# The second token group's up-projection as seven half-size products, in a fused attention and squared-ReLU kernel

## Chip, cores and metric

The kernel runs on one core of one Trainium2 chip. The metric is the device time of one execution in microseconds (us). TensorE (PE in the profile) does the matrix products, PEld is its loading of stationary operands, DVE is VectorE, ACT is ScalarE, POOL is GpSimd, SP is SyncE. POOL, SP and ACT also issue transfers (DMA).

## The reference

Attention with a linear distance bias and a window of 128 positions, then two dense layers with a squared ReLU between them:

```python
B, H, S, D = 8, 8, 576, 64
scores = matmul(q, k.T) / sqrt(D)                     # per batch and head
rel = pos[:, None] - pos[None, :]
scores = where((rel >= 0) & (rel < 128), scores - slope[h] * abs(rel), -1e9)
attn = softmax(scores)
x = (attn @ v).transpose(0, 2, 1, 3).reshape(4608, 512)
h = x @ w_in                                          # 512 -> 2048
g = maximum(h, 0) ** 2
out = g @ w_out                                       # 2048 -> 512, float32
```

## The kernel before

The 4608 tokens are nine groups of 512. A group is four blocks of 128 rows; a block is one batch and 128 positions (the last 64 positions of two batches share one). Matrices are bf16, sums are fp32 in PSUM, which has eight banks of 128 x 512 that all of PE's results share.

**Attention** of a block `m` is a chain of steps. `lk`, `lq`, `lv` (or `lkq`) load k, q and v by POOL. `tp m.0`, `tp m.1` transpose k and q on PE and `ev` evacuates them (from block 8 on, the transfer `kqT` does it on SP). `s m.0`, `s m.1` are the scores on PE, `e m.0` to `e m.3` the exponentials on ACT, `m m.0`, `m m.1` the multiplication with the mask on DVE, `pv m.0`, `pv m.1` the product with v on PE, `r` and `n` the reciprocal and the normalization on DVE, `xp m` the transposition of the result on PE and `x m` its evacuation (from block 13 on a transfer on SP). `mask*`, `pm*`, `one*`, `ident`, `dist*`, `slope*` are constants, built early.

**The up-projection** has two forms. The plain one (function `unit`, steps `u g.r.e`) multiplies w_in with the tokens: group 0 in four rows of 128 tokens, group 1 in two rows of 256 tokens and eight steps of two 128-column pieces each. Every step is followed by a ReLU on ACT (`relu`), which empties the PSUM bank, and a square (`sq`) on DVE or ACT.

The other form (`up_product`, steps `f g.u.p`) computes a group's 2 x 2 block product with seven half-size products instead of eight (Strassen's scheme in Winograd's form), for each quarter `u` of the columns. Products 1, 6, 7 and 4 add up in one bank, 2 has its own, 5 and 3 share one. Between them, partial sums are copied to SBUF (`s1`, `s2`, `s5` by `snap`, line 430 for ACT and 428 for DVE) and added (`c11`, `c22`, `c12`, line 1137, with the ReLU in the same instruction); the fourth result takes a plain ReLU after product 4. The scheme needs four sums of weight quarters for each `u` (`us u.0` to `us u.3`, line 1062; `us u.2` overwrites a part of w_in and so waits for every plain step) and four differences of the inputs for each group (`ut g.0` to `ut g.3`, line 1085). Products 1 and 2 read only the group's first 256 tokens, the others all 512.

**The down-projection** of each group (`product`, steps `p g.p.z`, line 1271) uses the same scheme on sums of g (`S1` to `S4`, line 1417) and of w_out (`ws`, line 1229); `s1_g`, `c11_g` and so on combine, `st` stores.

**Order.** Nothing is scheduled at run time. `ORDER` is a text with one item for each step: name, engine (`a` ACT, `d` DVE, `g` POOL, `s` SP, none for PE) and the numbers of the buffers it takes, PSUM banks for PE steps. Each engine executes its items in this order, waiting where an input or a buffer isn't there yet. `G_UP` says how many groups are plain:

```python
def ups(g):
    if g >= G_UP:
        return [("up", g, u, p) for u in range(4) for p in (1, 2, 6, 5, 7, 3, 4)]
    ...
    return [("unit", g, r, e) for r, (_, _, steps) in enumerate(UNITS[g]) for e in range(len(steps))]
...
tops = [x for gg in range(G_UP) for x in g_up[gg]]     # up_weight_sums: what us u.2 waits for
```

Of the kernel before, what the change touches and what calls it, by code (L numbers as in the profile page):

```python
# [69 lines left out]
reluu0.0.0:a:0 u0.2.0::6 mask0.3:a mask1.2:a mask0.1:a mask1.6:a e3.1:a u0.1.0::3 u0.1.1::0 pv3.0::1 pv3.1::5  # L70
u0.2.1::4 u0.0.2::7 squ0.0.0:d one1.2:d reluu0.1.0:a:0 mask0.2:a reluu0.2.0:a:1 one1.8:d r3.0:d squ0.1.0:d one1.7:d
r3.1:d n3.0:d n3.1:d xp3.0::5 x3.0:d one1.5:d reluu0.2.1:a:0 one1.6:d squ0.2.1:d squ0.2.0:d reluu0.1.1:a:2 mask1.5:a
mask1.4:a mask0.7:a mask0.5:a mask1.3:a mask1.0:a reluu0.0.2:a:3 u0.1.2::0 tp4.0::5 tp4.1::7 ev4.1.0:d squ0.0.2:d
u0.2.2::4 ev4.0.0:a reluu0.0.1:a:1 s4.0::7,2 s4.1::5,1 reluu0.1.2:a:0 e4.0:a lk5:g reluu0.2.2:a:3 lk6:g lq5:g lv5:g
lq6:g w_in4:g tp5.0::0 u0.0.3::6 u0.3.0::4 tp5.1::7 squ0.0.1:d one1.1:d one1.0:d squ0.1.2:d ev5.0.0:d e4.1:a mask0.0:a
mask0.4:a mask0.6:a m4.0:d ev5.1.0:d squ0.1.1:d lk7:g lv4:g lv6:g lq7:g w_out3:g w_out0:g lv7:g w_out2:g w_out1:g
e4.3:a reluu0.3.0:a:0 e4.2:a reluu0.0.3:a:1 squ0.3.0:d u0.3.1::2 tp6.0::7 reluu0.3.1:a:0 ev6.0.0:d tp6.1::4 s5.0::5,1
ev6.1.0:d one1.4:d one1.3:d squ0.0.3:d s5.1::6,0 u0.3.2::7 e5.0:a s6.0::5,4 s6.1::2,3 e5.1:a e5.3:a e6.0:a e5.2:a
# [5 lines left out]
u1.0.6::4 u1.0.4::2 reluu1.0.4:a:2 squ1.0.4:a u1.0.1::6 reluu1.0.0:a:1 squ1.0.0:a xp6.0::2 pv7.1::0 r7.1:d pv7.0::5
r7.0:d n7.0:d n7.1:d u1.0.7::1 u1.0.5::7 lkq8:g lkq12:g kqT8:s kqT12:s lkq9:g kqT9:s lkq10:g xp7.0::0 x7.0:a u1.0.3::5
S2.0.0:d x6.0:d reluu1.0.7:a:1 squ1.0.7:d us1.0:d us1.1:d us3.1:d reluu1.0.1:a:2 u1.1.6::0 reluu1.0.6:a:0
reluu1.1.6:a:1 squ1.0.6:a squ1.0.1:d us2.1:d reluu1.0.2:a:3 reluu1.0.3:a:0 squ1.0.2:a u1.1.3::1 u1.1.1::4 u1.1.4::0
reluu1.1.4:a:2 pm1:d pm2:d ws0.0:d squ1.0.3:a u1.1.5::5 u1.1.2::0 squ1.1.6:a reluu1.1.2:a:1 squ1.1.2:d S1.0.1:d
reluu1.1.3:a:0 S2.0.1:d squ1.1.4:a u1.1.0::3 u1.1.7::0 reluu1.1.1:a:1 squ1.1.1:a pm0:a us3.3:d us1.3:d reluu1.1.5:a:1
reluu1.1.0:a:2 squ1.1.5:a reluu1.0.5:a:3 squ1.0.5:a p0.2.0::1 p0.2.1 p1.1.0::4 p0.1.0::6 p1.1.1 p0.1.1 us0.2:d ws1.0:d  # L90
ws0.1:d ws0.3:d S3.0.1:d p0.5.0::7 ws0.2:d us2.3:d us0.3:d ws1.1:d ws1.3:d us2.2:d S4.0.1:d S4.0.0:d p0.5.1 squ1.1.0:d
S1.1.0:d ws1.2:d s1_0:a:0 p0.6.0 p0.6.1 s1_1:a:1 squ1.1.3:a s5_0:a:2 reluu1.1.7:a:0 squ1.1.7:a c11_0:d S2.1.0:d
us3.2:d S1.1.1:d us1.2:d s8.1::0,3 s8.0::5,2 s2_0:a:3 e8.0:a e8.3:a e8.1:a e8.2:a p0.3.0 p0.3.1 s9.1::3,1 s9.0::2,5
p0.7.0 p0.7.1 e9.0:a e9.3:a e9.2:a e9.1:a lv8:g lv9:g lv10:g kqT10:s s10.0::1,2 s10.1::3,0 lkq13:g lkq15:g lkq14:g
lv12:g lkq16:g lv13:g lv14:g kqT13:s kqT15:s c12_0:d S2.1.1:d m8.1:d m8.0:d c22_0:d p1.2.0::5 p1.2.1 m9.1:d e10.0:a
e10.1:a e10.3:a e10.2:a c11_1:d S3.1.0:d m10.1:d m9.0:d s12.1::0,2 s12.0::1,7 p0.4.0 pv8.0::5 pv8.1::3 r8.0:d r8.1:d
n8.0:d m10.0:d n8.1:d e12.0:a e12.3:a e12.1:a e12.2:a kqT14:s kqT16:s p1.6.0 p0.4.1 s3_0:a:4 pv9.0::2 pv10::7,5 r9.0:d
m12.1:d n9.0:d pv9.1::0 r9.1:d n9.1:d r10.0:d m12.0:d n10.0:d p1.6.1 xp8.0::2 p1.5.0::6 pv12.1::0 pv12.0::3 xp9.0::7
s2_1:a:5 p1.5.1 x8.0:a x9.0:a S3.1.1:d r12.1:d r10.1:d r12.0:d n12.0:d n10.1:d n12.1:d S4.1.1:d S4.1.0:d s13.0::3,7
s13.1::2,1 xp10.0::5 xp12.0::0 p1.7.0 p1.7.1 e13.0:a e13.1:a s5_1:a:6 e13.3:a e13.2:a m13.0:d x12.0:d x10.0:d ut2.0:d  # L100
s15.0::0,1 s14.0::7,3 s14.1::2,5 e15.0:a e14.0:a e15.1:a e14.2:a e14.1:a e14.3:a p1.3.0 p1.3.1 m13.1:d ut2.1:d c22_1:d
f2.0.5::1 pv13.1::2 pv13.0::3 m15.0:d c12_1:d ut2.2:d r13.0:d r13.1:d m14.0:d n13.0:d m14.1:d n13.1:d lkq17:g lv15:g
lv16:g lkq18:g st0.7.2:s st0.7.3:s st0.3.1:s kqT17:s st1.7.3:s st1.7.2:s st0.3.0:s s15.1::5,6 s16.0::7,0 e16.0:a
# [10 lines left out]
sqf2.3.4:a st1.2.1:s st0.2.0:s st1.3.1:s st0.2.1:s st1.2.0:s st1.3.0:s kqT18:s x14:s x13:s x15:s x16:s kqT20:s kqT21:s
kqT22:s s18.0::1,2 s18.1::0,7 p2.2.0::3 p2.2.1 S1.2.1:d S2.2.1:d r17.0:d S4.2.1:d S3.2.1:d r17.1:d n17.0:d e18.0:a
e18.1:a s1_2:a:3 S3.2.0:d n17.1:d m18.0:d p2.5.0::2 p2.6.0 p2.5.1 p2.6.1 f3.0.1::5 f3.0.2::4 f3.1.1::1 s2_2:d:7
e18.2:a e18.3:a s1.3.0:a:5 ut3.0:d ut3.1:d m18.1:d ut3.2:d c11.3.0:d:0 ut3.3:d c11_2:d f3.0.5::7 f3.0.6 s2.3.0:a:1
s5.3.0:a:0 s1.3.1:a:5 p2.7.0 f3.1.5::0 f3.0.7 s5.3.1:a:6 c22.3.0:d:3 f3.0.3 f3.1.6 s2.3.1:a:0 f3.1.3 s20.0::3,4
# [1362 lines left out]
```

## Time and profile before

| | |
|---|---|
| Time, median of 3 runs | 287.88 us (287.31 to 288.01) |
| The profiled execution, its own time | 288.0 us |
| Its span | 285.9 us, 8500 instructions |
| PE busy | 277.0 us (97%) |
| DVE busy | 247.1 us (86%) |
| ACT busy | 207.5 us (73%) |
| POOL busy | 106.3 us (37%) |
| DMA | 39.08 MB, mean 137 GB/s |

The span runs from the first to the last instruction; the rest of the time lies around it. The page gives the busy share of each engine, also in 40 equal slices of the span (one digit each, in tenths). Groups of instructions carry a count, the busy time of all, the mean duration of one in ns, and the idle time of the engine just ahead of them with what ended it. Consecutive instructions of an engine can overlap, so the distance between two starts is shorter than the duration.

### The profile page before, as it was taken

To read this page: it belongs to the slowest core of one execution; us is meant where nothing else is said; L and a number is where in the kernel's file an instruction comes from. 1 tells how busy PE (TensorE), PEld (TensorE's weight loads), DVE (VectorE), ACT (ScalarE), POOL (GpSimd) and SP (SyncE) were. 2 spreads that over 40 slices of the span, in tenths; PEclk is the share of its full clock that TensorE was granted. 3 is DMA by queue.
4 is the path that set the end of the run, shared out by engine and by line. 5 is a ranking of instruction groups with operands and counts; after the bars stand their busy time and mean duration, and the time that the engine had idled before them with its cause. 6 is when DMAs were issued, how large, how long until landed. Compare 5 with 4: busy or idle time off the path is not lost.

```text
span 285.9 us, 8500 instructions
## 1 busy us (share of the span) xinstructions
PE 277.0 (97%) x3403; PEld 240.0 (84%) x3404; DVE 247.1 (86%) x566; ACT 207.5 (73%) x408; POOL 106.3 (37%) x132
## 2 busy tenths in 40 slices
PE   6799999999999999999999999999999999999994
...
DVE  2555898799999999999999899998999979998752
ACT  4579978986588993879779958686898655657300
...
GB/s 126 161 197 167 183 201 165 171 172 148 206 145 250 131 172 129 149 207 130 203 135 150 139 174 164 170 164 157 148 93 39 40 73 3 0 111 39 53 79 127
DMA packets 169062, 39.08 MB, mean 137 GB/s; under 512 B 154560, under 2 KB 169024, under 8 KB 169024
## 3 DMA queue, kind: packets, MB, share of 16 engines
...
q1 hardware_dynamic: 53248, 20.00, 41.1%
q8 instruction: 26, 0.43, 0.7%
...
## 4 chain that ended last, share of the span: by engine, by line
PE 95%; ACT 2%; DVE 1%; issue 0%; POOL 0%; DVEq 0%; POOLq 0%
PE o L1271 38%; PE h L1116 30%; PE h L1021 9%; PE s L745 6%; PE pv L874 5%; PE wm L662 2%; PE xp L921 1%; PE tp L690 1%; ACT P L823 1%; ACT rt L988 1%; PE pv L856 1%; PE o L1373 0%; PE s L805 0%; ACT masks L475 0%; PE pv L851 0%; PE s L814 0%
## 5 line engine op out<-in xcount | busy, mean ns | idle before, releaser
L1271 PEld LDWEIGHTS <-g 128*128 128x128 bf16 x704 | 67.3, 98 | 9.0
L777 ACT ACTIVATE P<-s 128x512 bf16<-128x512 f32 x120 | 64.7, 613 | 5.7 <-PE s L745 3.3
L430 ACT ACTIVATE f<-h 128x512 f32<-128x512 f32 x74 | 42.5, 601 | 25.8 <-PE h L1116 25.5
L1137 DVE CUSTOM_DVE_ANT_0 rt<-h,f 128x512 bf16<-128x512 f32 x84 | 56.4, 684 | 4.9 <-ACT f L430 1.7
L980 ACT ACTIVATE g<-rt 128x512 bf16<-128x512 bf16 x79 | 48.4, 634 | 6.4 <-DVE rt L1137 5.9
L1271 PE MATMUL o<-w_out_sb,g 128*128 128x256 bf16 x432 | 52.3, 273 | 0.0
L1116 PE MATMUL h<-xT,w_in_sb 128*128 128x256 bf16 x336 | 46.9, 273 | 0.0
L1116 PEld LDWEIGHTS <-w_in_sb 128*128 128x128 bf16 x448 | 42.2, 98 | 5.6
L616 POOL DMA_DIRECT2D kq<-in_k_dram x24 | 21.5, 895 | 57.7 <-DMA kqT<-kq 54.7
L988 ACT ACTIVATE rt<-h 128x512 bf16<-128x512 f32 (+1 forms) x61 | 35.2, 599 | 8.6 <-PE h L1116 3.9
L1271 PE MATMUL o<-wsum,sums 128*128 128x256 bf16 x288 | 35.5, 273 | 0.0
L1116 PEld LDWEIGHTS <-us 128*128 128x128 bf16 x336 | 31.9, 98 | 4.3 <-DVE ut L1085 0.2
L1271 PE MATMUL o<-wsum,g 128*128 128x256 bf16 x272 | 34.5, 273 | 0.0
L772 DVE TENSOR_TENSOR P<-P,masks 128x1024 bf16<-128x1024 bf16 x48 | 32.2, 680 | 1.3 <-ACT masks L475 0.8
L1116 PE MATMUL h<-ut,us 128*128 128x256 bf16 x224 | 31.1, 273 | 0.0
L1021 PE MATMUL h<-xT,w_in_sb 128*128 128x128 bf16 (+1 forms) x384 | 30.8, 237 | 0.1
L982 DVE TENSOR_TENSOR g<-rt 128x512 bf16<-128x512 bf16 (+1 forms) x66 | 26.1, 413 | 4.7 <-ACT rt L988 4.4
L1271 PEld LDWEIGHTS <-sums 128*128 128x128 bf16 x288 | 27.5, 98 | 3.1
L901 DVE TENSOR_TENSOR x<-pv,rec 128x256 bf16<-128x256 f32 x72 | 28.7, 417 | 0.7
L1021 PEld LDWEIGHTS <-w_in_sb 128*128 128x128 bf16 x384 | 27.0, 98 | 2.3 <-issue 0.2
L621 POOL DMA_DIRECT2D vt<-in_v_dram x28 | 25.0, 908 | 7.8 <-PE pv L856 5.3
L430 ACT ACTIVATE f<-o 128x512 f32<-128x512 f32 x29 | 17.3, 599 | 11.0 <-PE o L1271 10.0
...
## 6 DMA issues: line engine op xcount, KB each, us to landing
...
w_out_sb<-in_moe_w_out_dram POOLq DMA_DIRECT2D x4, 512.0 KB, 11.6
w_in_sb<-in_moe_w_in_dram POOLq DMA_DIRECT2D x3, 512.0 KB, 8.6
...
```

The lines of the kernel that those rows point to most:

```text
L430: nc.scalar.activation(o, i, AF.Copy)
L621: nc.gpsimd.dma_start(tile_of(s_v[m])[0:n, :, 0:D], source(v, m))
L772: nc.vector.tensor_tensor(flat(Pt[sP.idx], w), flat(Pt[sP.idx], w), flat(mk, w), op=ALU.mult)
L777: nc.scalar.activation(flat(Pt[sP.idx], slice(2 * i, 2 * i + 2)), sS[i].tile.rearrange("p (j t) -> p j t", j=2)[:, :, lo:hi], AF.Exp, bias ...
L901: nc.vector.tensor_tensor(o, heads(sv)[0:n, :, 0:D], sr.tile[0:n, :].unsqueeze(2).to_broadcast([n, 4, D]), op=ALU.mult)
L980: nc.scalar.activation(o, i, AF.Square, bias=0.0, scale=1.0)
L982: nc.vector.tensor_tensor(o, i, i, op=ALU.mult)
L988: nc.scalar.activation(rts[srt.idx][:, 0:n], slot.tile[:, 0:n], AF.Relu, bias=0.0, scale=1.0)
L1021: nc.tensor.matmul(slot.tile[:, f * w:(f + 1) * w], w_in_sb[:, cc, fc * 128:(fc + 1) * 128], xT[:, cc, lo % (XR * 128):lo % (XR * 128) + w ...
L1116: nc.tensor.matmul(slot.tile[:, j * 256:j * 256 + 256], a, b_, start=fresh and j == 0 and c == 0, stop=c == 1, skip_group_check=True)
L1137: nc.vector._custom_dve(TENSOR_ADD_SAT, out=rts[srt.idx], in0=slot.tile, in1=other(), s0=FMAX, s1=0.0)
L1271: nc.tensor.matmul(slot.tile[:, z * 256:z * 256 + 256], stationary(c), moving(c), start=fresh and z == 0 and c == 0, stop=c == F - 1, skip ...
```

## The change

`G_UP` goes from 2 to 1: group 1's sixteen plain steps `u1.*` with their ReLUs and squares are replaced by the 28 products `f1.u.p` with their copies, sums, squares and the four input differences `ut1.*`; the weight sums `us` are needed before group 1's products, not before group 2's, and `us u.2` waits for group 0's plain steps only. The order is the same for the first 110 items and another one from there to the end, with other engines for some evacuations and squares and other banks.

```diff
-G_UP = 2
+G_UP = 1
...
 reluu0.0.0:a:0 u0.2.0::6 mask0.3:a mask1.2:a mask0.1:a mask1.6:a e3.1:a u0.1.0::3 u0.1.1::0 pv3.0::1
-pv3.1::5 u0.2.1::4 u0.0.2::7 squ0.0.0:d one1.2:d reluu0.1.0:a:0 mask0.2:a reluu0.2.0:a:1 one1.8:d r3.0:d squ0.1.0:d
-one1.7:d r3.1:d n3.0:d n3.1:d xp3.0::5 x3.0:d one1.5:d reluu0.2.1:a:0 one1.6:d squ0.2.1:d squ0.2.0:d reluu0.1.1:a:2
-mask1.5:a mask1.4:a mask0.7:a mask0.5:a mask1.3:a mask1.0:a reluu0.0.2:a:3 u0.1.2::0 tp4.0::5 tp4.1::7 ev4.1.0:d
-squ0.0.2:d u0.2.2::4 ev4.0.0:a reluu0.0.1:a:1 s4.0::7,2 s4.1::5,1 reluu0.1.2:a:0 e4.0:a lk5:g reluu0.2.2:a:3 lk6:g
-lq5:g lv5:g lq6:g w_in4:g tp5.0::0 u0.0.3::6 u0.3.0::4 tp5.1::7
...
-x5.0:d squ0.2.3:d pv6.1::0 r6.0:d squ0.3.2:d squ0.3.3:d S1.0.0:d s7.0::7,4 reluu0.1.3:a:1 r6.1:d e7.0:a e7.1:a m7.0:d
-us0.0:d s7.1::2,5 e7.3:a e7.2:a n6.0:d m7.1:d us3.0:d n6.1:d squ0.1.3:d us0.1:d S3.0.0:d us2.0:d u1.0.2::3 u1.0.0::7
...
+mask0.2:a reluu0.0.1:a:1 u0.2.1::2 pv3.1::5 lk5:g lq5:g one1.6:d mask0.4:a reluu0.1.0:a:2 squ0.1.0:d mask1.3:a
+mask0.5:a mask0.0:a u0.0.2::3 one1.1:d squ0.0.1:d one1.4:d one1.8:d one1.5:d mask1.4:a reluu0.2.0:a:3 mask1.5:a
+squ0.0.0:d r3.0:d r3.1:d n3.0:d n3.1:d reluu0.1.1:a:0 mask1.0:a reluu0.2.1:a:1 reluu0.0.2:a:2 mask0.6:a xp3.0::5
+u0.0.3::2 tp4.0::3 tp4.1::0 u0.1.2::1 w_in4:g lk6:g lk7:g lq6:g lv4:g lv5:g lv6:g lq7:g lv7:g ev4.0.0:a squ0.1.1:d
+squ0.2.0:d one1.2:d squ0.0.2:d squ0.2.1:d one1.3:d ev4.1.0:d x3.0:d s4.0::0,3 s4.1::5,6 tp5.0::4 ev5.0.0:d tp5.1::7
+reluu0.0.3:a:1 mask0.7:a reluu0.1.2:a:2 ev5.1.0:d squ0.0.3:d squ0.1.2:d e4.0:a e4.3:a e4.1:a m4.0:d u0.2.2::1 e4.2:a
+m4.1:d us0.0:d us1.0:d s5.0::6,7 s5.1::4,0 e5.0:a reluu0.2.2:a:2 e5.3:a e5.1:a u0.3.0::3 u0.3.2::6 reluu0.3.2:a:1
+e5.2:a reluu0.3.0:a:3 us3.0:d us2.0:d one1.0:d m5.0:d us1.1:d one1.7:d m5.1:d squ0.2.2:d us0.1:d u0.3.1::0 tp6.0::6
+tp7.0::7 tp6.1::1 u0.2.3::4 ev6.0.0:a ev6.1.0:a ev7.0.0:a reluu0.2.3:a:2 pv5.0::6 s6.0::1,3 pv5.1::5 tp7.1::7
+ev7.1.0:a e6.0:a e6.1:a pv4.1::4 pv4.0::2 r5.0:d us3.1:d n5.0:d r5.1:d squ0.3.0:d u0.0.4::6 r4.1:d n5.1:d r4.0:d
+n4.0:d squ0.3.2:d n4.1:d us2.1:d reluu0.0.4:a:3 m6.0:d S1.0.0:d squ0.0.4:d s7.0::1,5 s6.1::2,7 u0.1.3::3 s7.1::6,4
+e7.0:a e6.2:a e7.1:a m7.0:d e7.3:a e6.3:a m6.1:d xp4.0::1 pv6.0::2 u0.3.3::5 xp5.0::4 x4.0:a pv6.1::1 pv7.0::7 e7.2:a
+x5.0:a reluu0.1.3:a:3 reluu0.3.1:a:1 reluu0.3.3:a:0 w_out1:g w_out0:g lkq8:g lkq12:g w_out3:g w_out2:g kqT8:s kqT12:s
+lkq9:g lkq10:g lv8:g kqT9:s kqT10:s r6.0:d us0.2:d n6.0:d r6.1:d m7.1:d r7.0:d n6.1:d f1.1.2::4 f1.0.2::2 pv7.1::3
+n7.0:d r7.1:d squ0.3.3:d n7.1:d xp6.0::1 f1.1.1::0 f1.3.2::7 us1.2:d squ0.3.1:d x6.0:a s1.1.1:a:0 f1.3.1::3 xp7.0::1
+x7.0:a c11.1.1:d:0 f1.2.1::5 f1.0.1::6 f1.2.2::1 s1.1.2:a:0 s1.1.0:a:1 s1.1.3:a:2 us0.3:d ut1.0:d f1.0.5::4 ut1.1:d
+squ0.2.3:d f1.1.6 us2.2:d c11.1.0:d:2 ut1.2:d f1.0.6 sqc11.1.1:a s2.1.1:a:3 s2.1.0:a:1 s5.1.0:a:4 f1.3.6 f1.1.5::2
...
+f1.2.3 p0.1.0::2 f1.0.4 c22.1.2:d:2 S1.0.1:d S3.0.0:d reluf1.0.4:a:0 sqc22.1.2:a p0.1.1 sqf1.0.4:a c12.1.2:d:1
+c12.1.3:d:2 c22.1.3:d:0 S2.0.0:d f1.2.4 p0.5.0::6 p0.5.1 p1.1.0::7 s1_0:a:6 sqc12.1.2:a sqc22.1.3:a reluf1.2.4:a:1
...
```

More of the change, by code (lines that the diff above doesn't have):

```diff
@@ L69 @@
 n2.1:d u0.0.1::2 r1.0:d r1.1:d n1.0:d n1.1:d xp2.0::6 s3 u0.0.0::0 xp1.0::3 dist0:d x2.0:a e3.0:a x1.0:a mask1.7:a
[L70 to L78, printed above, removed]
@@ L84 @@
[L84 to L93, printed above, removed]
@@ L94 @@
[L94 to L103, printed above, removed]
@@ L114 @@
[L114 to L118, printed above, removed]
@@ L169 @@
-e37.2:a p5.3.0 p5.3.1 pv35.1::7 f6.3.1::4 f6.3.2::2 c22_5:d c12_5:d r35.1:d n35.1:d f6.2.1::3 s38.1::7,5 s38.0::0,1
-m37.0:d s1.6.3:a:2 e38.0:a e38.1:a e38.3:a c11.6.3:d:0 sqc11.6.3:d m37.1:d m38.0:d s1.6.2:d:2 p5.4.0 f6.3.6 f6.2.2::0
-f6.3.5::1 pv37.0::5 pv37.1::2 c11.6.2:d:0 s2.6.3:a:3 f6.3.7 r37.1:d f6.2.6 p5.4.1 f6.2.5::0 e38.2:a s5.6.3:a:1
-c22.6.3:d:2 m38.1:d r37.0:d n37.0:d n37.1:d s2.6.2:a:2 sqc11.6.2:a f6.2.7 f6.3.3 st4.4.3:s x31:s x32:s st5.2.1:s
-st5.2.0:s st4.3.0:s x33:s st4.3.1:s st4.4.2:s x34:s s5.6.2:a:1 c22.6.2:d:0 f6.2.3 sqc22.6.3:a sqf6.0.4:a c12.6.2:d:2
@@ L199 @@
-st8.4.1:s st8.4.0:s st8.3.0:a c21.1.128_8:d st8.4.1b:a
+reluu0.0.0:a:0 u0.2.0::6 mask0.3:a mask1.2:a mask0.1:a mask1.6:a e3.1:a u0.1.0::3 u0.1.1::0 pv3.0::1 mask0.2:a
+reluu0.0.1:a:1 u0.2.1::2 pv3.1::5 lk5:g lq5:g one1.6:d mask0.4:a reluu0.1.0:a:2 squ0.1.0:d mask1.3:a mask0.5:a
+mask0.0:a u0.0.2::3 one1.1:d squ0.0.1:d one1.4:d one1.8:d one1.5:d mask1.4:a reluu0.2.0:a:3 mask1.5:a squ0.0.0:d
+r3.0:d r3.1:d n3.0:d n3.1:d reluu0.1.1:a:0 mask1.0:a reluu0.2.1:a:1 reluu0.0.2:a:2 mask0.6:a xp3.0::5 u0.0.3::2
@@ new lines @@
+tp4.0::3 tp4.1::0 u0.1.2::1 w_in4:g lk6:g lk7:g lq6:g lv4:g lv5:g lv6:g lq7:g lv7:g ev4.0.0:a squ0.1.1:d squ0.2.0:d
+one1.2:d squ0.0.2:d squ0.2.1:d one1.3:d ev4.1.0:d x3.0:d s4.0::0,3 s4.1::5,6 tp5.0::4 ev5.0.0:d tp5.1::7
+reluu0.0.3:a:1 mask0.7:a reluu0.1.2:a:2 ev5.1.0:d squ0.0.3:d squ0.1.2:d e4.0:a e4.3:a e4.1:a m4.0:d u0.2.2::1 e4.2:a
+m4.1:d us0.0:d us1.0:d s5.0::6,7 s5.1::4,0 e5.0:a reluu0.2.2:a:2 e5.3:a e5.1:a u0.3.0::3 u0.3.2::6 reluu0.3.2:a:1
+e5.2:a reluu0.3.0:a:3 us3.0:d us2.0:d one1.0:d m5.0:d us1.1:d one1.7:d m5.1:d squ0.2.2:d us0.1:d u0.3.1::0 tp6.0::6
@@ new lines @@
+pm2:d r8.1:d r8.0:d m10.0:d S2.1.1:d s3_0:a:2 e12.0:a e12.3:a e12.2:a e12.1:a p1.5.0::2 pv9.1::0 p1.5.1 p1.6.0
+pv9.0::4 p1.6.1 s5_1:a:4 s2_1:a:3 m10.1:d S3.1.1:d m12.0:d r9.0:d n9.0:d r9.1:d n8.0:d n9.1:d pv12.0::1 pv10::4,3
+n8.1:d r12.0:d r10.0:d r10.1:d n10.0:d S4.1.1:d n10.1:d m12.1:d n12.0:d xp9.0::0 p1.7.0 kqT14:s x9.0:a s13.0::0,4
+s13.1::5,6 p1.7.1 e13.0:a e13.2:a e13.1:a pv12.1::0 xp10.0::3 xp8.0::5 x10.0:a e13.3:a x8.0:a r12.1:d n12.1:d m13.0:d
+p1.3.0 xp12.0::3 pv13.0::0 s15.0::6,4 s14.0::5,1 e14.0:a e15.0:a e14.1:a e15.1:a c22_1:d x12.0:d r13.0:d ut2.0:d
@@ new lines @@
+s5.2.3:a:7 f2.2.3 s17.1::0,3 f2.3.7 kqT18:s st0.3.1:s st1.7.3:s st0.2.0:s st1.3.0:s x14:s st1.7.2:s st0.2.1:s
+st0.3.0:s kqT20:s x15:s kqT22:s x16:s kqT21:s sqc22.2.2:d c22.2.3:d:2 sqc22.2.1:a c12.2.2:d:1 f2.3.3 p2.1.0::2
+c12.2.3:d:0 sqc12.2.2:d e17.3:a reluf2.2.4:a:3 sqf2.2.4:d e17.2:a sqc22.2.3:a f2.3.4 reluf2.3.4:a:2 sqf2.3.4:a p2.1.1
+pv17.0::4 sqc12.2.3:a s18.1::1,5 s18.0::0,6 e18.0:a e18.2:a s1_2:a:5 e18.1:a p2.2.0::3 p2.2.1 S1.2.0:d S2.2.0:d
+S1.2.1:d r17.0:d S2.2.1:d n17.0:d c11_2:d m17.1:d S3.2.1:d S3.2.0:d p2.5.0::1 p2.6.0 f3.0.1::3 s1.3.0:a:0 e18.3:a
```

191 lines of the change are left out of this document (103 added, 88 removed).

## The prediction

> **What bounds the kernel now.** I read the page first, then the stretches of time, the chain that ended last, the groups by shape and the timeline of the first 65 us.
>
> ```profile
> span 285.9 us, 8500 instructions
> PE 277.0 (97%) x3403; PEld 240.0 (84%) x3404; DVE 247.1 (86%) x566; ACT 207.5 (73%) x408; POOL 106.3 (37%) x132
> PE   6799999999999999999999999999999999999994
> DVE  2555898799999999999999899998999979998752
> ACT  4579978986588993879779958686898655657300
> ```
>
> The profiled execution took 288.0 us, 2.1 us of it outside the span; the median of the three runs is 287.88. TensorE is full from the fifth slice to the end, and VectorE nearly so from the ninth (56 us). Before that ACT has the fuller slices, the fifth and the sixth.
>
> ```profile
> 20.30:38.70 18.40, 17.95 (x358) 16.88 (x356) 13.97 (x48) 17.46 (x43) 12.51 (x15) 1.00 1.87 179
> 38.70:53.70 15.00, 15.00 (x153) 13.44 (x153) 11.90 (x31) 12.09 (x25) 7.61 (x10) 1.00 1.87 174
> 53.70:281.80 228.10, 228.10 (x2713) 199.21 (x2711) 212.64 (x454) 166.22 (x315) 68.48 (x82) 1.00 1.21 129
> 60.00:80.00 20.00, 20.00 (x302) 17.06 (x301) 19.71 (x45) 14.68 (x29) 14.13 (x19) 1.00 1.98 169
> ```
>
> The columns are length, then busy time of PE, PEld, DVE, ACT and POOL. The first stretch begins where the new order begins, the second holds the plain up-projection of group 1, the third starts with the first down product. From 53.7 on PE has no idle time at all. So whatever PE work goes is gained in full, and whatever PE waits is lost in full; nothing later makes it good. In the first stretch ACT is busy 95% and DVE 76%: what PE can meet there is ACT.
>
> ```profile
> 20.60 0.91 PE h L1021 x16
> 21.53 1.08 ACT rt L988 x2
> 22.61 1.18 ACT masks L475 x6
> 23.80 0.50 ACT rt L988
> 24.33 0.38 PE tp L690 x4
> ...
> 28.28 0.22 PE tp L690 x4
> 28.50 0.89 PE h L1021 x16
> ...
> 31.54 0.55 PE s L745 x16
> ...
> 33.98 0.97 PE pv L874 x32
> ...
> 38.67 4.47 PE h L1021 x40
> ...
> 53.77 8.73 PE o L1271 x80
> ```
>
> The chain leaves PE only once behind 20 us for longer: from 21.5 to 24.3 it runs over relus and six masks on ACT, because a transpose takes the PSUM bank that a relu behind those masks frees. From 38.67 (u1.0.2) it is PE alone. Eighty 256-column matmuls in 8.73 us make 109.1 ns each.
>
> **The change, part by part.**
>
> ```profile
> L1021 PE MATMUL h<-xT,w_in_sb 128*128 128x256 bf16 x128 | 14.6, 273 | 0.0
> L1137 DVE CUSTOM_DVE_ANT_0 rt<-h,f 128x512 bf16<-128x512 f32 x84 | 56.4, 684 | 4.9 <-ACT f L430 1.7 <-PE h L1116 1.1 <-ACT g L980 0.9
> L430 ACT ACTIVATE f<-h 128x512 f32<-128x512 f32 x74 | 42.5, 601 | 25.8 <-PE h L1116 25.5
> L988 ACT ACTIVATE rt<-h 128x512 bf16<-128x512 f32 x59 | 34.6, 607 | 8.6 <-PE h L1116 3.9 <-PE h L1021 2.0 <-DVE rt L1137 1.5
> L988 ACT ACTIVATE rt<-h 128x256 bf16<-128x256 f32 x2 | 0.8, 386 | 0.0
> ```
>
> *1. PE work.* Group 1's 128 plain matmuls go; 4 quarters of 7 products of 4 matmuls, 112, come, of the same shape. 16 x 109.1 ns = **1.75 us less**, all of it on the path.
>
> *2. Work on the other engines.* Relus of group 1 fall from 16 to 4, and 12 copies of partial sums into f (L430, 601 ns against 607) come: ACT is even. DVE gets 12 sums (L1137) and 4 input differences (ut). What an instruction costs in a row of its kind is the distance between starts:
>
> ```profile
> 19.94 0.60 ACT L988 ACTIVATE rt<-h 128x512 bf16<-128x512 f32 x1
> 20.19 0.41 PE L874 MATMUL pv<-vf,P 128*128 128x65 bf16 x8
> 44.24 0.76 DVE L901 TENSOR_TENSOR x<-pv,rec 128x256 bf16<-128x256 f32 x2
> 46.36 2.06 ACT L988 ACTIVATE rt<-h 128x512 bf16<-128x512 f32 x4
> 89.51 1.28 DVE L1137 CUSTOM_DVE_ANT_0 rt<-h,f 128x512 bf16<-128x512 f32 x2
> 97.73 0.75 DVE L982 TENSOR_TENSOR g<-rt 128x512 bf16<-128x512 bf16 x2
> ```
>
> ACT 512 wide: (2.06 - 0.61)/3 = 0.48 us. A mask: 1.18/6 = 0.20, from the chain above. DVE sum: 1.28 - 0.68 = 0.60; DVE 512 in bf16, and the norm: 0.75 - 0.42 = 0.33. So 12 x 0.60 + 4 x 0.33 = 8.5 us more on DVE, less five squares and a few evacuations that the new order gives to ACT (about 4 us). DVE's 86% rises by about 1.5 points. It must bear this, and the 16 weight sums (us) brought forward, between 30 and 60 us, where the second row of the stretches shows it 3.1 us idle.
>
> *3. The new order up to the first of group 1.* The shared 110 steps end with ACT free at 19.94 (row above) and PE at the second half of the pv row, 20.35. From there I walk the two lists. PE's next is u0.2.1 in bank 2, then pv3.1, u0.0.2, xp3, and **u0.0.3, again in bank 2**, which the relu of u0.2.1 has to free. PE's own work up to there is 0.12 + 2 x 0.89 + 0.22 = 2.1 us: it arrives at 22.5. ACT has ahead of that relu eight masks (1.6), three relus (1.44) and a half-wide one (estimate 0.27, from 386 against 607 ns): it starts at 23.25, lasts 0.61, and PE goes on at 23.95. **A wait of 1.45 us**; before, PE's idle time in the whole first stretch, this jam included, is 18.40 - 17.95 = 0.45 us.
>
> Queued behind u0.0.3 are tp4.0 and tp4.1, so ACT itself runs dry: free at 24.4, its next step evacuates tp4.0, which ends at 23.95 + 0.89 + 0.38 = 25.2. ACT restarts at 25.35. From there to x5.0, which evacuates the last input that products 1 and 2 read and frees the bank of f1.1.2, ACT's list holds 5 evacuations, 7 relus, 16 exponentials, x4.0 and a mask: 29 x 0.48 + 0.2 = 14.1 us, until 39.45; two short waits that the walk meets (0.15 for the relu of u0.3.2, 0.40 for the evacuation of tp7.1); x5.0 itself 0.60 and the way to PE 0.1. **f1.1.2 starts at 40.7.** In the old order x5 is DVE's, and u1.0.2 starts at 38.67 with the same PE steps behind it but for one half of values (8 matmuls, 0.24).
>
> *4. From there to the down products.* Before the first down product both orders put the same PE steps, but for 16 units of 8 matmuls (13.97 us) against 25 of the 28 products of 4 (10.91). From f1.1.2 on the new list has 11.6 us until then; ut1.0 waits for x7.0, and that for pv7.1, n7.1 and xp7.0, for which I add 0.3. First down product at 52.6, and the three products left over (1.31) make it the equal of 53.9. Before: 53.77. **So waits of some 1.9 us more eat the 1.75: +0.2.**
>
> *5. Switches to score matmuls.*
>
> ```profile
> 61.25 1.25 PE L1271 MATMUL o<-wsum,sums 128*128 128x256 bf16 x10
> 62.43 0.23 PE L745 MATMUL s<-kqT,kqT 64*128 64x128 bf16 x2
> ...
> 62.84 0.22 PE L745 MATMUL s<-kqT 64*128 64x128 bf16 x2
> 62.99 1.92 PE L1271 MATMUL o<-w_out_sb,g 128*128 128x256 bf16 x16
> ```
>
> Ten matmuls from 61.25 end at 62.34, the scores start at 62.43; on the way back the last pair at 62.84 would let the next start at 62.90, and it starts at 62.99. About 0.09 each way, 0.18 a visit. The old list visits scores 32 times, the new one 33: +0.2. [...]
>
> *6. Transfers.* In POOL's queue w_in4 moves ahead of three loads (lk6, lv5, lq6), and lkq8 and lkq12 ahead of w_out3 and w_out2.
>
> ```profile
> 22.58 0.75 POOL L543 DMA_DIRECT2D w_in_sb<-in_moe_w_in_dram  x1 [1.40 <-DMA w_in_sb<-in_moe_w_in_dram]
> 47.38 1.34 SPq L676 DMA_TRANSPOSE kqT<-kq  x1
> ...
> w_in_sb<-in_moe_w_in_dram POOLq DMA_DIRECT2D x3, 512.0 KB, 8.6
> ```
>
> Now it lands about 22.58 + 8.6 = 31.2. In the new list us0.0 reads it from about 29.5 us. Three places sooner are at least 3 x 0.8 us (106.3 us of POOL for 132 instructions): it lands by 28.8, and the step costs nothing; were it late, m5.0 stands behind us0.0 on DVE and pv5.0 behind that, 1.7 us at the old landing. kqT8 waits for all weights; four issues later are 3.2 us, 50.6 instead of 47.4, and the scores that read it run at 62.4 (row above) or later: 0. The order behind p0 moves without changing work, and the tail (last product, three sums, stores) is the same list: 0, if PE waits there as little as now.
>
> **Sum:** 288.0 + 0.2 (waits 1.95, work -1.75) + 0.2 (the visit) = **288.4 us**; against the median of 287.88 that is half a microsecond more. About 0.3% (0.86 us) is what a measurement of this kernel tells from no change, so this is none.
>
> **Rivals.** *A, faster: the walk overstates ACT.* Had ACT no idle time, x5.0 would start at 19.94 + 34 x 0.48 + 0.27 + 10 x 0.20 = 38.5 and f1.1.2 at 39.2, 1.5 us sooner: **286.9**. For it: 17.46 of 18.40 us busy now. Against: tp4.0 really stands behind u0.0.3.
>
> *B, slower: DVE becomes the pacer between m6.1 and p0.3.0.* That stretch of DVE's list is 12 sums, 6 S, 4 ws and 2 masks (24 x 0.60), 8 us, 4 ut, 4 squares and 4 norms (20 x 0.33) and 4 reciprocals: 21.4 us. m6.1 can start when e6.3 ends, 39.4, so S4.0.1 is there at 60.9; PE wants it 9.2 us behind its first product, at 61.8. The margin is 0.9 us. At the idle share of 60 to 80 us (1.5%) 0.3 us goes and nothing happens. It decides from 4% on; at 10%, half of what 38.7 to 53.7 shows (21%), 2.4 us go: **289.9**, and at 21% it would be some 293.
>
> *C, slower: waits further back.* The order is new as far as the end, and nothing in this trace shows it; the old one has PE without idle time from 53.7. Two or three waits at the size of the old order's early idle time (0.45) give **289.5**.
>
> *D: the products are not cheaper,* because a half-size product came with more per matmul: **290.1**. Against: groups 2 to 8 run them at 109 ns.
>
> **How the numbers follow.** Forecast 0.52 (its own range 287.6 to 289.2: 0.4 us either way for each of the two walked waits), A 0.14, B 0.20, C 0.12, D 0.02. Faster by over 0.3% (under 287.0): most of A, 0.12. Slower by over 0.3% (over 288.7): B, D, most of C and a fifth of the forecast, 0.43. Within: 0.45. The range runs from A to just behind B, 286.7 to 290.3.
>
> **What would show it.** Right: 896 matmuls where the products are issued (784 now), none of 256 columns among the plain ones; a PE wait near 22.5 to 24 that ends on ACT rt; f1's first matmul near 40.7 and the first down product near 52.6; no idle PE later. Wrong: f1 before 39.5 (A); p0.5, p0.6 or p0.3 (PE o from sums or g) waiting for a DVE sum between 55 and 62 (B); PE waits behind 62 (C).

## The result, and the profile after

The changed kernel took 290.01 us in the median (288.27 to 292.91), the kernel before 287.95 beside it (287.22 to 289.62): a ratio of 1.0056 with a 95% interval of 1.0033 to 1.0079, 0.56% slower (the execution of 292.91 us counts as slow and is not in the ratio). The forecast of 288.4 was 1.6 us too low; the time lies in its range, near its upper end. Repeated later, the ratio was 1.0061 (1.0032 to 1.009). No run of the changed kernel was under 288.27, and they spread over 3 us and more.

The profiled execution took 289.69 us. Its page, with the slices of PE and of its granted clock:

```profile
span 287.9 us, 8490 instructions
PE 278.3 (97%) x3388; PEld 239.9 (83%) x3388; DVE 250.4 (87%) x570; ACT 213.4 (74%) x420; POOL 106.3 (37%) x132
PE   6898999999999999999999999999999999999994
PEclk9979999999999999999999999999999999999999
```

The third slice of the clock shows a 7 (a 9 before). The stretches of time around it; behind the length of the stretch stands PE's busy time, and the third number from the end is the granted clock:

```profile
12.00:13.00 1.00, 0.49 (x10) 0.30 (x8) 0.60 (x2) 1.00 (x3) 1.00 (x2) 1.00 1.58 168
13.00:14.00 1.00, 0.53 (x12) 0.40 (x12) 0.62 (x4) 0.61 (x2) 1.00 (x3) 1.00 1.44 190
14.00:15.00 1.00, 0.52 (x10) 0.33 (x7) 0.81 (x3) 0.87 (x2) 1.00 (x3) 1.00 1.42 198
15.00:16.00 1.00, 1.00 (x17) 1.00 (x17) 0.51 (x3) 0.30 (x2) 1.00 (x2) 0.50 1.28 206
16.00:17.00 1.00, 1.00 (x8) 0.45 (x6) 1.00 (x6) 0.00 (x0) 1.00 (x2) 0.50 1.24 207
17.00:18.00 1.00, 1.00 (x12) 0.98 (x10) 0.97 (x5) 0.00 (x0) 0.49 (x1) 0.50 1.74 177
18.00:19.00 1.00, 1.00 (x18) 0.72 (x16) 0.04 (x1) 0.71 (x2) 0.00 (x0) 0.80 1.76 203
```

From 15.0 to about 18.4 us the clock was 0.50 (the mean of 0.80 in the last row makes 0.4 us at 0.50). That lies in the first 110 steps, which both kernels share: u0.1.1, one of the last of them on PE, ended at 22.12 us instead of 20.35 (an expectation below has 20.38 for it). So this profile is 1.8 us late before anything that the change touched begins. Behind that point, three rows of PE's timeline:

```profile
24.84 0.40 PE L924 MATMUL xp<-ident,x 128*128 128x128 bf16 x4 [0.42 <-DVE x L904]
25.68 1.05 PE L1024 MATMUL h<-xT,w_in_sb 128*128 128x128 bf16 x16 [0.45 <-ACT rt L991]
...
281.88 1.93 PE L1376 MATMUL o<-wsum,g 128*128 128x256 bf16 x24
```

The up-products in the groups by shape:

```profile
L1119 PE MATMUL h<-xT,w_in_sb 128*128 128x256 bf16 x384 | 53.4, 273 | 0.1
L1119 PE MATMUL h<-ut,us 128*128 128x256 bf16 x256 | 34.4, 273 | 0.0
L1119 PE MATMUL h<-xT,us 128*128 128x256 bf16 x128 | 19.2, 273 | 0.0
L1119 PE MATMUL h<-ut,w_in_sb 128*128 128x256 bf16 x128 | 18.7, 273 | 0.0
```

384 + 256 + 128 + 128 are the 896 product matmuls. The wait at u0.0.3 (25.68) is there, ended by the ReLU on ACT. The changed kernel's second profile (290.21 us) has no clock dip and is the one to read. From its PE timeline:

```profile
23.39 0.83 PE L1024 MATMUL h<-xT,w_in_sb 128*128 128x128 bf16 x12 [0.45 <-ACT rt L991]
...
34.23 0.40 PE L693 MATMUL tp<-ident,kq 128*128 128x128 bf16 x4 [0.59 <-DMA kq<-in_q_dram]
...
40.70 1.03 PE L1119 MATMUL h<-xT,w_in_sb 128*128 128x256 bf16 x8
...
112.70 1.48 PE L1119 MATMUL h<-ut,us 128*128 128x256 bf16 x12 [2.08 <-DVE ut L1088]
...
282.42 1.93 PE L1376 MATMUL o<-wsum,g 128*128 128x256 bf16 x24
```

From the chain of work that ended last in it:

```profile
26.03 8.16 DMA kq<-in_q_dram
34.23 0.40 PE tp L693 x4
...
35.16 1.08 ACT P L780 x2
36.24 0.49 ACT rt L991
36.73 2.45 ACT P L780 x5
39.18 0.49 ACT xT L433
39.67 0.49 ACT P L780
40.16 0.50 ACT xT L433
...
106.50 0.26 DVE x L904
106.76 5.34 DMA xT<-x
...
112.22 0.44 DVE ut L1088
...
112.70 2.83 PE h L1119 x24
```

And from SP's timeline, the issues of x15, kqT22 and x16:

```profile
100.46 2.49 SPq L911 DMA_TRANSPOSE xT<-x  x1
103.12 3.54 SPq L679 DMA_TRANSPOSE kqT<-kq  x1
106.76 1.22 SPq L911 DMA_TRANSPOSE xT<-x  x1
```

Two waits here were not in the prediction. tp7.1 waits 0.59 us for the load lq7, which lands at 34.19, and the chain from there runs over ACT to f1.1.2 at 40.70, the last 5.5 us of it on ACT without a break. The load alone is not the difference: in the kernel before lq7 landed no sooner (34.58), PE did not wait for it, and group 1 started 4.0 us behind it, here 6.5. And far behind, f3.0.5 waits 2.08 us: its input difference ut3.0 needs the transposed x of block 16. The last row of SP is that transfer, x16. Its input was ready at 100.2 (n16.1's end), but SP had kqT20, x15 and kqT22 ahead of it and issued it at 106.76; it landed at 112.10. In the old list x13 to x16 stand ahead of kqT20, n16.1 ends at 95.55, x16 is issued at 97.5 and lands at 103.35, some 7 us before ut3.0 starts at 110.55. So two things came together: x16's input is ready 4.6 us later (100.2 against 95.55), and its issue comes another 6.6 us behind that. (The DVE x ahead of it in the chain is n17.0, which ends at 106.89, behind that issue, and is not its input.)

The names of the lower rows belong to the experiments below. With these two points each profiled execution can be split at the first matmul of group 1 (u1.0.2 or f1.1.2) and at the end of the last product, in us. Column 3 counts from the end of u0.1.1, column 4 from group 1's first matmul; column 5 is the wait at f3.0.5 within column 4:

| kernel | end of u0.1.1 | to group 1 | to the end of PE | wait f3.0.5 | its time |
|---|---|---|---|---|---|
| before | 20.35 | 18.26 | 243.20 | 0 | 288.0 |
| changed, first profile | 22.12 | 20.19 | 241.50 | 0 | 289.69 |
| changed, second profile | 19.83 | 20.87 | 243.64 | 2.08 | 290.21 |
| masks later | 20.22 | 20.93 | 243.21 | 1.65 | 290.24 |
| x15, x16 ahead | 19.74 | 21.30 | 241.50 | 0 | 288.43 |
| x15, x16, lq7 ahead | 20.43 | 19.63 | 241.49 | 0 | 287.31 |
| before, with dummies | 20.01 | 18.26 | 243.20 | 0 | 287.31 |
| changed, with dummies | 20.59 | 20.38 | 241.48 | 0 | 288.33 |

The stretch behind group 1's start, without that wait, is 241.5 to 241.6 us in every kernel with the new order and 243.2 with the old one. The gain is there each time, 1.6 to 1.7 us. It goes again in three places: a start of group 1 that is 1.9 to 3.0 us later behind u0.1.1 (1.4 with lq7 ahead), a wait of about 2 us for x16 in some executions, and the clock, which hits both kernels (3.4 us at 0.50 in the first profile of the changed one, and in one of the kernel before with x16 moved).

### The profile page after: what moved, and what is told of

It is laid out like the page before. It is cut to its first block, busy times and chain, and to the rows that moved or that the text cites. A ratio compares the mean times of both kernels' runs of the same rounds, so it can differ in the third digit from the quotient of the medians.

```text
span 287.9 us, 8490 instructions
## 1 busy us (share of the span) xinstructions
PE 278.3 (97%) x3388; PEld 239.9 (83%) x3388; DVE 250.4 (87%) x570; ACT 213.4 (74%) x420; POOL 106.3 (37%) x132
## 4 chain that ended last, share of the span: by engine, by line
PE 92%; ACT 5%; DVE 1%; issue 1%; POOL 0%; DVEq 0%; POOLq 0%; ACTq 0%
PE o L1274 38%; PE h L1119 35%; PE s L748 6%; PE pv L877 4%; PE h L1024 3%; PE wm L665 2%; ACT P L780 1%; PE tp L693 1%; ACT masks L478 1%; PE xp L924 1%; ACT P L826 1%; ACT rt L991 1%; PE s L808 1%; ACT xT L433 1%; PE pv L859 1%
## 5 line engine op out<-in xcount | busy, mean ns | idle before, releaser
L1140 DVE CUSTOM_DVE_ANT_0 rt<-h,f 128x512 bf16<-128x512 f32 x96 | 64.0, 684 | 4.8 <-PE h L1119 2.9
L433 ACT ACTIVATE f<-h 128x512 f32<-128x512 f32 x87 | 50.1, 604 | 18.1 <-PE h L1119 14.4
L983 ACT ACTIVATE g<-rt 128x512 bf16<-128x512 bf16 x84 | 51.8, 634 | 6.6 <-DVE rt L1140 6.1
L1119 PE MATMUL h<-xT,w_in_sb 128*128 128x256 bf16 x384 | 53.4, 273 | 0.1
L1119 PEld LDWEIGHTS <-w_in_sb 128*128 128x128 bf16 x512 | 47.7, 98 | 6.6 <-DVE x L904 0.5
L1119 PEld LDWEIGHTS <-us 128*128 128x128 bf16 x384 | 36.9, 98 | 4.7 <-DVE ut L1088 0.2
L1119 PE MATMUL h<-ut,us 128*128 128x256 bf16 x256 | 34.4, 273 | 0.0
L991 ACT ACTIVATE rt<-h 128x512 bf16<-128x512 f32 (+1 forms) x49 | 28.5, 601 | 5.8 <-DVE g L985 2.9
L877 PEld LDWEIGHTS <-P 128*128 128x128 bf16 x448 | 20.6, 99 | 3.2 <-ACT P L826 1.3
L619 POOL DMA_DIRECT2D kq<-in_q_dram x24 | 21.8, 910 | 1.6 <-DMA w_out_sb<-in_moe_w_out_dram 1.6
```

The source lines that it names most:

```text
L433: nc.scalar.activation(o, i, AF.Copy)
L619: nc.gpsimd.dma_start(view(kq[s_kq[m].idx], i), source(src, m, split))
L877: nc.tensor.matmul(sv.tile[0:n, hi * (D + 1):(hi + 1) * (D + 1)], prob, tile_of(s_v[mk])[:, h, 0:D + 1], start=mk == parts[0][1], stop=mk ...
L983: nc.scalar.activation(o, i, AF.Square, bias=0.0, scale=1.0)
L991: nc.scalar.activation(rts[srt.idx][:, 0:n], slot.tile[:, 0:n], AF.Relu, bias=0.0, scale=1.0)
L1119: nc.tensor.matmul(slot.tile[:, j * 256:j * 256 + 256], a, b_, start=fresh and j == 0 and c == 0, stop=c == 1, skip_group_check=True)
```

## The experiments

**The changed kernel once more**, unedited.

> The changed kernel once more, nothing edited. In its first profiled execution the common prefix (the first 110 steps, up to u0.1.1) ended 1.74 us later than in the one of before (22.12 against 20.38), behind a granted clock of 0.50 from 15.0 to 18.4 us, and from there to the last product both took nearly the same (261.69 against 261.42 us). Theory 'clock' (the extra is the dip in the prefix, which the change only meets more often): this profile's time is 288.3 to 288.6 us if no dip is in it and 289.5 to 290 if one is, and prefix end to last product is again 261.7, within 0.2. Theory 'waits' (the new order's own waits make it slower): no dip, and still 289.5 or more, with over 262.8 us behind the prefix.

Median 289.65 us (288.62 to 292.43), before 288.23 beside it. No dip, and still 290.21 us in the profile: "clock" alone fell, "waits" held, with 264.5 us from u0.1.1 to the end of the last full product, 2.1 of it at one place that neither theory had named.

**The masks later on ACT.** Two squares on DVE, squ0.0.0 and squ0.0.1, come sooner as well; the lines show ACT's and PE's items.

```diff
-... mask0.4:a reluu0.1.0:a:2 squ0.1.0:d mask1.3:a mask0.5:a mask0.0:a u0.0.2::3 ... mask1.4:a reluu0.2.0:a:3 mask1.5:a
-... reluu0.1.1:a:0 mask1.0:a reluu0.2.1:a:1 reluu0.0.2:a:2 mask0.6:a xp3.0::5 u0.0.3::2
+... reluu0.1.0:a:2 squ0.1.0:d u0.0.2::3 ... reluu0.2.0:a:3 mask0.4:a ... reluu0.1.1:a:0 reluu0.2.1:a:1 mask1.3:a
+reluu0.0.2:a:2 mask0.5:a mask0.0:a mask1.4:a mask1.5:a mask1.0:a mask0.6:a xp3.0::5 u0.0.3::2
```

> The changed kernel with six of the masks on ACT behind the ReLU that frees u0.0.3's bank (and the two squares that free its buffers ahead on DVE); the work is the same. My theory of the early jam: u0.0.3 waits 0.2 us instead of 1.2 to 1.45, tp4.0 ends 1.2 us sooner and ACT no longer runs dry ahead of it; f1.1.2 and the first down product come 0.9 to 1.2 us sooner, and the time falls by 0.9 to 1.2 us against the changed kernel, to about 287.4 in undisturbed executions. Rival (ACT's total work, not its order, sets f1.1.2): the wait goes, but f1.1.2 stays within 0.3 us of the changed kernel's place behind the prefix. Theory 'clock' expects the spread between runs to stay.

Median 290.28 us (288.58 to 292.51): no gain. PE's timeline has u0.0.3 without a wait:

```profile
22.77 0.89 PE L1025 MATMUL h<-xT,w_in_sb 128*128 128x128 bf16 x13
```

The chain that ended last:

```profile
26.10 8.54 DMA kq<-in_q_dram
...
41.16 1.03 PE h L1120 x8
```

u0.0.3 came 2.55 us behind u0.1.1 instead of 3.56, a whole microsecond sooner, and f1.1.2 20.93 behind it instead of 20.87. PE met lq7's landing (34.64) all the same and waited there 0.67 us, and f1.1.2 came 6.5 us behind that landing as before. My theory of the early jam fell as a cause of the time: the jam is real, but a load stands behind it.

**Dummy products in PE's idle stretches**, in the changed kernel and in the one before. The dummies write a bank that the step behind them overwrites.

```diff
+BUSY = {'tp1.0': 3, 'pv2.0': 6, 'pv0.0': 8, 'xp0.0': 7}
...
     def fill(task, slot):
-        for _ in range(int(task.gap * FILL / 56.0) if task.gap > 400.0 else 0):
+        for _ in range(BUSY.get(task.name, 0)):
             nc.tensor.matmul(slot.tile[:, 0:128], warm[:, 0:128], warm[:, 0:128], start=True, stop=True)
```

> The changed kernel with 24 dummy products of 128 columns in four idle stretches of PE between 9.9 and 14.5 us (3, 6, 8 and 7 of them, ahead of tp1.0, pv2.0, pv0.0 and xp0.0, written into banks that the step behind them overwrites), so that PE is not idle there. Theory 'clock': the granted clock stays at 1.00 up to 280 us in every execution, the spread of 3 us falls to under 1, and the median falls from 290.0 to 288.3 to 288.6. Theory 'waits': the median stays at 289.5 to 290.

> The kernel before with the same 24 dummy products. Theory 'clock': its few slow runs (289.2 to 289.6 of 11) go and the median stays at 287.7 to 288.0, so that the changed kernel with dummies is 0.3 to 0.7 us slower than this one, as predicted. Theory 'waits': no change here, and the difference to the changed kernel with dummies stays at 1.6 us or more.

Changed: 288.89 us (288.33 to 289.98). Before: 287.79 (287.31 to 288.69). In 70 runs of the kernel before that stood beside these and the next experiments, 17 had a mean clock of 0.994, and those took 289.27 to 291.35 us; with the dummies none of the 24 was under 0.997. So with dummies in PE's idle stretches between 10 and 15 us the dip was not seen, and it makes most of the slow tail of the kernel before, 17 of its 19 executions above 289.2 us; the changed one reached 290.87 us with a clock of 1.00. The difference between the two with dummies is 1.1 us, between what the two theories expected. Without the dip and without dummies it is larger: the changed kernel's 15 executions of both measurements with a mean clock of 0.996 or more have a median of 289.69 us, the 26 of the kernel before beside the repeat 287.85. So the clock is part of the spread and no cause of the difference. That the dummies took 0.76 us from the changed kernel (289.65 to 288.89) is not shown to be the clock: in its profile x16 lands at 107.84 and f3.0.5 has no wait.

**x15 and x16 ahead on SP.**

```diff
-st1.7.2:s st0.2.1:s st0.3.0:s kqT20:s x15:s kqT22:s x16:s kqT21:s
+st1.7.2:s st0.2.1:s x15:s st0.3.0:s x16:s kqT20:s kqT22:s kqT21:s
```

> The changed kernel with two steps moved in SP's list alone: x15 ahead of one store and kqT20, x16 ahead of kqT20 and kqT22. In the second profile of the changed kernel x16 is ready at 100.2 us (n16.1), is issued at 106.76 behind them, lands at 112.10, and f3.0.5 waits 2.08 us for it (1.65 in the one with the masks moved; none in the two others, where it landed at 107.8 and 110.2). Theory 'transfer of x16' (this late wait is what makes the changed kernel slower): x16 is issued near 101 and lands by 109.5, no PE wait is left behind 62 us in any execution, and the median falls from 289.7 by 0.8 to 1.6 us, to 288.1 to 288.9, within 0.5 us of before. Rival (the wait only moves on, to the next transfer that kqT20 and kqT22 now delay, or to DVE): f3.0.5 no longer waits, but another PE wait of 1 us or more stands between 110 and 135, and the median stays at 289.3 or more.

Median 288.36 us (287.79 to 289.72) against 287.89 beside it, a ratio of 1.0002 (0.9978 to 1.0026): no slowdown is shown any more, though the median is 0.47 us higher. SP's timeline:

```profile
98.20 1.19 SPq L911 DMA_TRANSPOSE xT<-x  x1
99.44 0.58 SPq L1313 DMA_DIRECT2D out_dram<-f  x1
100.55 1.79 SPq L911 DMA_TRANSPOSE xT<-x  x1
102.45 7.43 SPq L679 DMA_TRANSPOSE kqT<-kq  x4
```

PE's timeline:

```profile
110.88 1.48 PE L1119 MATMUL h<-ut,us 128*128 128x256 bf16 x12
...
280.61 1.93 PE L1376 MATMUL o<-wsum,g 128*128 128x256 bf16 x24
```

x16 is issued at 100.55 and lands at 107.10, f3.0.5 (110.88) has no wait, and none came in its place; the four transposes behind it were early enough. Of four profiles with the old place of x16 two have the wait, of the seven with x16 ahead (this and the later runs) none. The two medians, 289.65 and 288.36, come from different series of runs; against the kernel before beside each, the excess fell from 1.42 to 0.47 us, and among executions with a mean clock of 0.996 or more from 1.77 (289.62 against 287.85) to 0.48 (288.30 against 287.82). So two steps of one queue's list made 1.0 to 1.3 us.

**x16 behind the transposes in the kernel before.**

```diff
-x16:s kqT20:s kqT21:s kqT22:s
+kqT20:s kqT21:s kqT22:s x16:s
```

> The kernel before with one step moved in SP's list: x16 behind kqT20, kqT21 and kqT22 instead of ahead of them. Theory 'transfer of x16': it is issued near 105 to 107 instead of 97.5, lands at 111 to 112.5, where ut3.0 wants it at 110.1, so that f3.0.5 waits 1 to 2 us in some of the executions and the median is 0.7 to 1.8 us above before. Rival (the stretch has slack for it): no wait at f3.0.5 and a median within 0.4 us of before.

Median 288.23 us (287.47 to 291.36) against 287.89, a ratio of 1.0008 (0.9982 to 1.0034): the rival's slack. x16 was issued at 106.42 and landed at 110.67. The profiled execution has the clock dip and wants ut3.0 only near 112, so it can't show whether an execution without one just misses it. In this one the three transposes cut the margin from 7 us to 1.7 (landing at 110.67, ut3.0 at 112.33). What made up the rest in the new order, the later n16.1 or slower transfers, is not shown.

**x ahead, masks later, and lq7 ahead on POOL.** The stores and x are as in the run before last.

```diff
-lq6:g lv4:g lv5:g lv6:g lq7:g
+lq6:g lv5:g lq7:g lv4:g lv6:g
```

> The changed kernel with x15 and x16 ahead as in the other run, the masks later on ACT as in the earlier run, and lq7 ahead of lv4 and lv6 in POOL's list (lv5 first). In the undisturbed profiles so far tp7.1 waits 0.6 us for lq7's landing at 34.2 to 34.6, and f1.1.2 follows 6.5 us behind it, with the masks moved or not. Theory 'two causes in a row' (ACT's jam and lq7's landing each set f1.1.2 if the other is gone): lq7 lands near 32.5, no PE wait at tp7.1, f1.1.2 comes 20.0 us or less behind the end of the prefix (20.9 before), and the median is 0.7 to 1.2 us under the kernel with x ahead alone, 287.1 to 287.9. Rival (ACT's work sets it in any order): f1.1.2 stays 20.6 us or more behind the prefix, and the median within 0.4 us of the kernel with x ahead alone.

> The same three moves, and the 24 dummy products of 128 columns in the idle stretches of PE between 9.9 and 14.5 us. If the theories on the clock, on x16, on lq7 and on the masks all hold: no granted clock under 1.00 ahead of the last product, no PE wait over 0.3 us behind 42 us, a spread under 1 us, and a median of 286.4 to 287.2, 0.6 to 1.4 us faster than the kernel before with the same dummies (287.8). If only those on clock and x16 hold: 287.6 to 288.4.

288.71 us (287.99 to 290.20), and with dummies 289.02 (288.63 to 289.56): neither faster than x ahead alone, and the second outside both expectations. In the first, f1.1.2 came 20.46 behind u0.1.1, between the two expectations. Its chain:

```profile
25.06 8.12 DMA vt<-in_v_dram
33.17 0.14 issue
33.31 0.42 PE pv L877 x8
```

lq7 landed at 32.28, but lv4, now behind it, at 33.17, and pv5.0 started 0.14 us behind that. One load had taken the other's place. In the profile with dummies lv4 landed at 33.72, and ACT, which ran from 25.28 to 33.79 almost without a break, ended last ahead of pv5.0: with the masks later, a load and ACT's list end within 0.1 us of one another there.

**ACT relieved ahead of f1.1.2**, on top of that, without and with dummies.

```diff
-ev4.0.0:a ... e6.2:a e7.1:a m7.0:d e7.3:a e6.3:a m6.1:d xp4.0::1 pv6.0::2 u0.3.3::5 xp5.0::4 x4.0:a ... e7.2:a x5.0:a
+ev4.0.0:d ... e6.2:a e6.3:a m6.1:d e7.1:a m7.0:d e7.3:a xp4.0::1 pv6.0::2 xp5.0::4 u0.3.3::5 x4.0:a x5.0:a ... e7.2:a
```

> The kernel with x15 and x16 ahead, lq7 ahead and the masks later, with ACT relieved ahead of f1.1.2: ev4.0.0 given to DVE, e6.3 two places sooner, xp5.0 ahead of u0.3.3 and x5.0 ahead of e7.2. In the kernel without these moves ACT ran without a break from 35.15 to x5.0 at 40.15, f1.1.2 came 20.52 us behind the end of the prefix, and PE waited 1.05 us at 33.3 and 0.46 at 40. Theory 'ACT sets the start of f1': f1.1.2 comes 19.6 to 20.0 us behind the prefix, the wait of 0.38 ahead of pv6.1 goes, and the median is 0.4 to 0.9 us under that kernel, 287.5 to 288.0, level with before or just under it. Rival 'the loads set it' (lv4 and lq7 land at 33.2 and 32.3 at best): f1.1.2 moves by 0.4 us at most, 20.1 to 20.5 behind the prefix, and the median by less than 0.4.

> The same with the 24 dummy products in PE's early idle stretches. Theory 'clock': no execution over 289.2 and a spread under 1.2 us. Theory 'ACT sets the start of f1': 0.4 us or more under the kernel with dummies and without ACT relieved (289.0), so 288.6 or less; rival 'the loads set it': within 0.3 us of it.

288.77 us (288.26 to 290.34) and 289.20 (288.61 to 290.17). f1.1.2 came 20.93 and 20.94 us behind u0.1.1, outside both expectations, and the moves bought a new wait of 0.77 us at xp5.0, which now stands ahead of u0.3.3. ACT is not cleared by this: in the first profile the chain runs over ACT from 25.07 to 33.76 and again from 35.66 to 39.69, and PE waits 1.21 us at 33.83 for one of its ReLUs. So the run does not separate ACT from the loads. With dummies the medians of these kernels with x ahead are 0.3 to 0.4 us higher than without (288.71 and 289.02, 288.77 and 289.20), within overlapping intervals, so here the dummies are not shown to help.

**lq7 ahead of lv6 alone**, with x ahead, without and with the masks later.

```diff
-lv4:g lv5:g lv6:g lq7:g
+lv4:g lv5:g lq7:g lv6:g
```

> The changed kernel with x15 and x16 ahead, and one more step moved: lq7 one place sooner in POOL's list, ahead of lv6 alone, so that lv4 and lv5 keep their places (in the kernels with lv5 and lq7 ahead of lv4, pv5.0 started 0.14 us behind lv4's landing, at 33.3 to 33.9, 0.8 us or more later than in the kernel with x ahead alone, which took back what lq7 gave). Theory 'the loads set the start of f1': lq7 lands near 33.4 instead of 34.2 to 34.5, PE does not wait at tp7.1, pv5.0 stays near 32.9, and f1.1.2 comes 20.2 to 20.5 us behind the prefix instead of 20.9; the median falls by 0.3 to 0.6 us against the kernel with x ahead alone, to 287.8 to 288.1. Rival 'ACT sets it': the wait at tp7.1 goes and f1.1.2 stays 20.8 to 21.0 behind.

> The same with the masks later on ACT, too. Theory 'the loads set the start of f1': with u0.0.3 1 us sooner PE comes to the landings of lq6, lv5 and lq7 (31.2, 32.5, 33.4) earlier and waits there; f1.1.2 is at most 0.3 us sooner than without the masks moved, 19.9 to 20.5 behind the prefix. Rival 'the early jam counts once the loads are out of the way': 19.4 to 19.8 behind the prefix, and a median of 287.2 to 287.6, under before.

287.72 us (287.31 to 290.09) and 287.82 (287.41 to 288.93), with 288.35 for before beside them: ratios of 0.9996 (0.997 to 1.0023) and 0.9986 (0.9963 to 1.0008). The chain of the first:

```profile
24.74 7.93 DMA vt<-in_v_dram
32.71 0.39 PE pv L877 x7
...
34.52 1.08 ACT P L780 x2
...
40.06 1.03 PE h L1119 x8
```

tp7.1 no longer waits, the chain now comes from lv5's landing (32.67), and f1.1.2 starts at 40.06 instead of 41.04 with x ahead alone, 1.0 us sooner for one load moved by one place. Behind u0.1.1 that is 19.63 us instead of 21.30, but here u0.1.1 itself had waited 0.84 us for weights, so 1.0 is the fairer figure. The loads did set when ACT's last 5.5 us ahead of group 1 began. With the masks later f1.1.2 came 20.74 behind u0.1.1 in the one profile, outside both expectations, because lq5 landed at 27.22 there and tp5.1 waited 1.16 us for it: the loads again, at another place. Neither version is shown to beat the kernel before; both are level with it.

## Why the prediction was right and wrong, step by step

1. **PE work: right.** 1.7 us less behind group 1's start (waits taken out), the same within 0.1 in every profile. Group 1's own matmuls take 12.31 us from start to start for 112 against 14.07 for 128, 1.76 instead of the forecast 1.75. Of the 1.7 us, 0.12 is the half of values that the new order has ahead of f1.1.2; the products of the later groups take 0.23 more in the new order.
2. **More work on DVE: no part in it.** No PE wait behind f1.1.2 was for a DVE sum as such; rival B did not come. Its price set the upper end of the range, 290.3, so that the measured 290.01 lies inside is luck.
3. **The walk: right to 0.1 us by luck, with half of the mechanism.** u0.0.3 came 3.56 us behind u0.1.1 in both profiles, walked 3.6; the wait of 1.45 us shows there as two, 0.42 at xp3 for DVE's x and 0.45 at u0.0.3. f1.1.2 came at 40.70 in the second profile, walked 40.7; but u0.1.1 ended at 19.83 there and not at 20.35, so that behind it f1.1.2 came 20.87 us, walked 20.35. ACT does run without a break to x5.0, as walked, but only for the last 5.5 us; when that begins was set by lq7's landing, which the walk did not have. Moving the masks took away the jam and f1.1.2 stayed, and moving lq7 brought it 1.0 us forward. Where the clock dip made PE 1.8 us late, the same loads were hidden: group 1 then started 20.19 behind u0.1.1 instead of 20.87. That fits what the dip costs at the end of PE: the kernel before 1.8 us (283.60 with x16 behind, against 281.80) and the changed one 1.3 (283.81 against 282.54 with x ahead).
4. **The first down product: right in place.** 52.39 in the second profile, walked 52.6, but again with a u0.1.1 that ended 0.5 us sooner than walked. The old order's 38.67 and 53.77 are pieces of the chain, which begin where the piece ahead ends; the matmuls themselves start at 38.61 and 53.60. The net of steps 1, 3 and 5, forecast as +0.4, came out at 0.5 to 1.1: with x16 ahead the median is 0.47 over the kernel before, with dummies in both 1.10, and PE's end in these profiles 0.74 (282.54 against 281.80) and 0.98 later (282.45 against 281.47).
5. **The visits to score matmuls** are equal behind group 1's start (28 in both), so the extra one lies ahead of it, within step 3's waits; not separated by any run.
6. **Transfers, set to 0: the step that failed.** I looked at w_in4 and kqT8 and not at the order of SP's list behind the first down product, nor at the landing of lq7 against tp7.1. They were worth 0.6 us at tp7.1 and 0 to 2.1 at f3.0.5. The sentence "The order behind p0 moves without changing work" was true, and it moved x16 behind kqT20 and kqT22, and its input 4.6 us later.

Rival C, waits further back, is what came, with 0.12: not as two or three waits of 0.45 but as one of 2.1 us; that its 289.5 lies near the measured time is luck. Of the reasons given there, only "nothing in this trace shows it" was to the point. Its price should have come from the transfers, 5.2 to 9.0 us from issue to landing for x13 to kqT22 in the kernel before, and not from PE's early idle time.

What stays open: why the transposes of x between 85 and 125 us took up to 8.9 us from issue to landing in the changed kernel's second profile, which waited (6.6 in the median), and up to 7.6 in its first, which did not (4.9), with the same list on SP; how much of the lasting 0.5 us is the extra score visit; and what the dummies changed in the changed kernel besides the clock.
